# Units, weights and masks at the start of a fused decay-attention and softplus FFN kernel: a new order of loads, a mask on VectorE, a decay table made on the chip

## The chip, the cores and the metric

The kernel runs on one core of a Trainium2 chip. The metric is device time in microseconds (us) of one execution. The engines are TensorE (PE, with its weight loads PEld), VectorE (DVE), ScalarE (ACT), GpSimd (POOL) and SyncE (SP), which here issues nearly all DMAs. Each engine works through its own queue in order, and waits on semaphores where an instruction needs another engine's result or a transfer.

## What is computed

```python
# q, k, v: float32 [4, 8, 768, 64];  w_in: float64 [512, 2048];  w_out: float64 [2048, 512]
gamma = 1.0 - 2.0 ** (-5.0 - np.arange(H))
for t in range(S):
    state = gamma * state + einsum('bhd,bhe->bhde', k[:, :, t], v[:, :, t])
    y[:, :, t] = einsum('bhd,bhde->bhe', q[:, :, t], state) / sqrt(D)
x = y.transpose(0, 2, 1, 3).reshape(3072, 512)
h = x @ w_in
out = (max(h, 0) + log1p(exp(-abs(h)))) @ w_out
```

The attention has a per-head decay and no softmax. The FFN is two matmuls with a softplus between them. The weights come as 64-bit floats and are turned into float32 on the chip.

## The kernel before

**Units.** The attention is done in chunks of 128 tokens, and a unit is one chunk of one batch for four of the eight heads: `units` has 48 of them, unit n being half n % 2 of chunk n // 2. A unit passes through `load_unit` (three loads: q, k, v), `decay` (GpSimd multiplies q and v by decay tables), `operands` (transposes on TensorE, copies to `kz` and `qs`), `scores_whole` or `scores_first`/`scores_second`, the causal `mask`, `new_state` and `stack_and_outputs`, which writes the unit's part of x as a high and a low half (`xh`, `xl`) for the FFN. Units under `WHOLE` = 12 use plain float32 operands and load q and k by tokens; the later units load q and k in 32-token blocks and split them in high and low halves. For a unit under 12 the mask is a copy of the scores from PSUM to `a` on ScalarE (line 268), and then an `affine_select` on GpSimd (line 260).

**Ticks.** `PARTS` says at which tick of a unit each part is traced; unit n is shifted by 16 n. `tick(n)` traces all parts that are due. So unit n is loaded at tick 16 n - 24, its scores are traced at 16 n + 8 (later units at 16 n + 14 and 16 n + 17), and its outputs at 16 n + 20 (26).

**FFN.** A pair is 256 tokens (four units). `turns` and `steps` say which pairs meet which of the 16 blocks of 128 hidden columns: pair 0 with blocks 0 to 7, two blocks a step (steps 0 to 3), pair 1 with all 16 (steps 4 to 11), then pairs 0 and 2 together, and so on. A step is `hidden` (three matmuls for each of the four input tiles: lines 436 to 438), a softplus (lines 444 to 453, over VectorE, ScalarE, VectorE, ScalarE and GpSimd), and two steps later (`LAG`) `second` (lines 471 to 473). Steps 0 to 11 (`ordered`) are ordered by the planner, which works with a cost model of its own; from step 12 on the order on TensorE is the program's.

**Weights.** `load_weights(f)` loads block f of w_in and of w_out, 512 KB each, from SyncE. `convert_weights(f)` turns both into float32 and splits that in two: line 85 on ScalarE, 93 on VectorE or 91 on ScalarE, 94 and 95 on VectorE, the cast of line 97 on ScalarE, the low half of line 98 on GpSimd. The middle result `wp` has one PSUM buffer (tag `acc2`). From block `FETCH` = 3 on, a load is paced: it waits for the cast of the block three before, w_in's for w_in's and w_out's for w_out's. Before the ticks of pair 0 begin, units 0 and 1 are loaded; then the initial loop traces ticks -24 to 79, with block 0's loads in it at the start, block 1's after tick 12, block 2's after 28, and from tick 44 on a conversion and a load every 16 ticks. After that `convert_to` is called around each step.

**Buffers.** The tokens of v have a ring of three buffers, `vns` (unit n takes n % 3). q and k of units 2 and 3 use slots that the softplus takes over later (tags `gh`, `gl`). `attention_bank` gives the transposes, scores and outputs of units under 12 in turn one of two PSUM banks, `acc3` and `a`; later units have only `a`, and the FFN takes `acc3` from pair 2 on.

**Decay tables.** `qtabs` and `vtabs` hold token decays for each chunk and head, the first chunk's loaded and the others made from it (`token_decays`). `qblocks` is the same as `qtabs` in the layout of the later units. Its first chunk is loaded by 16 small DMAs of 0.5 KB (line 538, `block_decays`, called at step `TURN` = 4), and the other chunks are made by ten GpSimd multiplies (line 544).

## Time and profile before

| | us |
|---|---|
| median of three timed runs | 660.43 (659.85 to 660.67) |
| the profiled execution | 661.7 |
| its span, first to last instruction | 660.0 |
| TensorE busy | 648.3 |
| VectorE busy | 411.9 |
| ScalarE busy | 366.7 |
| GpSimd busy | 319.3 |

A timeline row reads: start in us, duration in us, engine, line, operation, what it writes and reads, shape, count; in brackets the idle time of the engine before it and what ended that. A row of the windows view gives a stretch, its length, the busy time of each engine in it, the granted share of TensorE's clock (PEclk), and what the DMA engines did. SPq and ACTq are the engines' sequencers, which issue DMAs. The ends of matmuls are modelled, so a busy TensorE need not be one at its peak.

### The profile page before, as it was taken

The page shows a single profiled execution, that of the slowest core. Times are in us where ns is not written, and L with a number is a line of the kernel's source. Part 1 is how long each engine was busy: PE and PEld are TensorE (multiplying, and loading weights), DVE is VectorE, ACT ScalarE, POOL GpSimd, SP SyncE. Part 2 cuts the span into 40 slices and gives each one's busy share as a digit, 9 for nine tenths or more (in the row PEclk, how much of TensorE's full clock was granted, in tenths as well). Part 3 has the DMA queues.
Part 4 walks back from the last instruction along what each step waited for, and adds up shares of the span by engine and source line. Part 5 has one row for each costly group of instructions (what it writes and reads, how often), then busy time and mean ns, then how long its engine had stood idle before and what let it go on. Part 6 is the DMA issues. An engine that isn't in the chain of part 4 may idle for free.

```text
span 660.0 us, 11777 instructions
## 1 busy us (share of the span) xinstructions
PE 648.3 (98%) x3762; PEld 555.2 (84%) x3762; DVE 411.9 (62%) x756; ACT 366.7 (56%) x799; POOL 319.3 (48%) x330
## 2 busy tenths in 40 slices
PE   7999999999999999999999999999999999999997
PEld 6898899888888888888888888888888888888896
DVE  5777888875685576576566665676677567522221
ACT  5867876656564555556565655565565555422221
POOL 5777758564445445444543464355345543332221
PEclk9999999999999999999999999999999999999999
DMA  9898573132223241131232132131222200000000
GB/s 241 227 260 239 161 195 86 37 76 41 42 62 62 39 96 21 26 84 35 40 84 37 35 92 35 17 82 29 46 61 48 41 19 33 0 1 33 0 33 32
DMA packets 153822, 46.69 MB, mean 71 GB/s; under 512 B 140448, under 2 KB 148640, under 8 KB 153760
## 3 DMA queue, kind: packets, MB, share of 16 engines
q1 hardware_dynamic: 153312, 45.93, 29.3%
q8 instruction: 29, 0.48, 0.3%
q14 instruction: 33, 0.27, 0.1%
q10 hardware_dynamic: 448, 0.01, 0.0%
HBM read 39.60 MB, written 6.29 MB: 70 GB/s over the span
## 4 chain that ended last, share of the span: by engine, by line
PE 92%; DMA 2%; ACT 2%; POOL 1%; issue 0%; DVE 0%; SPq 0%; POOLq 0%; ACTq 0%
PE hp L436 13%; PE hp L438 13%; PE acc L471 13%; PE acc L472 13%; PE hp L437 13%; PE acc L473 13%; PE yp L355 6%; PE sc L280 3%; PE stp L307 2%; DMA win<-in_moe_w_in_dram 2%; PE yp L345 1%; PE sc L267 1%; DMA vn<-in_v_dram 1%; PE yp L342 1%; PE tp L232 0%
## 5 line engine op out<-in xcount | busy, mean ns | idle before, releaser
L453 POOL TENSOR_TENSOR gl<-sp,gh 128x512 fp32r<-128x512 f32 x96 | 129.4, 1349 | 122.5 <-ACT gh L451 118.2
L436 PE MATMUL hp<-xh,winhl 128*128 128x512 f32 (+1 forms) x448 | 166.1, 371 | 1.0 <-DVE sp L449 0.5
L438 PE MATMUL hp<-xh,winhl 128*128 128x512 f32 (+1 forms) x448 | 162.0, 362 | 0.5 <-POOL winhl L98 0.5
L437 PE MATMUL hp<-xl,winhl 128*128 128x512 f32 (+1 forms) x448 | 161.7, 361 | 0.0
L445 ACT ACTIVATE sp<-sp 128x512 f32<-128x512 f32 x96 | 60.7, 632 | 167.7 <-DVE sp L444 167.6
L471 PE MATMUL acc<-wouthl,gh 128*128 128x512 f32 x384 | 151.0, 393 | 0.0
L472 PE MATMUL acc<-wouthl,gh 128*128 128x512 f32 x384 | 150.3, 391 | 0.0
L473 PE MATMUL acc<-wouthl,gl 128*128 128x512 f32 x384 | 149.0, 390 | 0.0
L444 DVE TENSOR_SCALAR sp<-hp 128x512 uint32<-128x512 uint32 x96 | 66.3, 690 | 84.8 <-PE hp L438 62.4
L438 PEld LDWEIGHTS hp<-xh,winhl 128*128 128x128 f32 x448 | 84.5, 189 | 14.3 <-POOL winhl L98 0.9
L436 PEld LDWEIGHTS hp<-xh,winhl 128*128 128x128 f32 x448 | 84.6, 189 | 12.3 <-PE yp L345 0.7
L437 PEld LDWEIGHTS hp<-xl,winhl 128*128 128x128 f32 x448 | 84.8, 189 | 11.2
L451 ACT CAST gh<-sp 128x512 fp32r<-128x512 f32 x96 | 59.7, 621 | 52.1 <-PE acc L472 40.0
L449 DVE SCALAR_TENSOR_TENSOR sp<-hp,sp 128x512 f32<-128x512 f32 x96 | 65.2, 680 | 33.7 <-ACT sp L445 33.2
L260 POOL TENSOR_SCALAR_AFFINE_SELECT a<-a 128x512 f32<-128x512 f32 x48 | 36.6, 762 | 101.6 <-DVE a L281 97.1
L473 PEld LDWEIGHTS acc<-wouthl,gl 128*128 128x128 f32 x384 | 71.8, 188 | 15.1
L471 PEld LDWEIGHTS acc<-wouthl,gh 128*128 128x128 f32 x384 | 72.1, 188 | 12.4
L472 PEld LDWEIGHTS acc<-wouthl,gh 128*128 128x128 f32 x384 | 72.4, 189 | 12.0
L213 POOL TENSOR_TENSOR vn<-vn,vtabs 128x256 f32<-128x256 f32 x48 | 29.8, 621 | 83.6 <-DMA vn<-in_v_dram 71.8
L281 DVE TENSOR_REDUCE a<-sc 128x256 f32<-128x512 f32 x72 | 49.3, 685 | 4.3 <-PE sc L280 3.5
L292 POOL TENSOR_TENSOR al<-a,ah 128x512 fp32r<-128x512 f32 x36 | 47.9, 1331 | 3.1 <-ACT ah L291 3.1
L329 DVE TENSOR_TENSOR st<-stp,st 64x128 fp32r<-64x128 f32 x60 | 17.3, 289 | 44.8 <-ACT st L327 44.2
(94 smaller groups left out, 919.3 us busy)
## 6 DMA issues: line engine op xcount, KB each, us to landing
win<-in_moe_w_in_dram SPq DMA_DIRECT2D x16, 512.0 KB, 4.9
wout<-in_moe_w_out_dram SPq DMA_DIRECT2D x16, 512.0 KB, 4.4
vn<-in_v_dram SPq DMA_DIRECT2D x48, 128.0 KB, 2.8
out_dram<-o SPq DMA_DIRECT2D x24, 256.0 KB, 2.1
vn<-in_k_dram SPq DMA_DIRECT2D x30, 128.0 KB, 2.4
kb<-in_k_dram SPq DMA_DIRECT2D x208, 16.0 KB, 1.7
qb<-in_q_dram SPq DMA_DIRECT2D x208, 16.0 KB, 1.7
qn<-in_q_dram SPq DMA_DIRECT2D x12, 128.0 KB, 4.9
```

The source lines that it names most:

```text
L281: summed[n] = nc.vector.tensor_reduce(sums[n][:, 2 * j:2 * j + 2, :], sc.rearrange("p h t c -> p h c t"), axis=mybir.AxisListType.X, op=AL ...
L436: nc.tensor.matmul(to, lhsT=wt[:, 0, d, :], rhs=xh[:, d], start=d == 0, stop=False)
L437: nc.tensor.matmul(to, lhsT=wt[:, 0, d, :], rhs=xl[:, d], start=False, stop=False)
L438: nc.tensor.matmul(to, lhsT=wt[:, 1, d, :], rhs=xh[:, d], start=False, stop=d == ND - 1)
L444: nc.vector.tensor_scalar(sp.bitcast(U32), hps[s].bitcast(U32), 0x80000000, None, op0=ALU.bitwise_or)
L445: nc.scalar.activation(sp, sp, AF.Softplus)
L449: nc.vector.scalar_tensor_tensor(g, hps.pop(s), 0.0, g, op0=ALU.max, op1=ALU.add)
L451: nc.scalar.copy(gh, g)
L453: nc.gpsimd.tensor_tensor(gl, sps.pop(s), gh.bitcast(F32), op=ALU.subtract)
L471: nc.tensor.matmul(to, lhsT=gh[:, k, ts], rhs=wt[:, 0], start=first, stop=False)
L472: nc.tensor.matmul(to, lhsT=gh[:, k, ts], rhs=wt[:, 1], start=False, stop=False)
L473: nc.tensor.matmul(to, lhsT=gl[:, k, ts], rhs=wt[:, 0], start=False, stop=last)
```

## The change

Seven edits:

1. Units 0 to 2 are loaded first, then the first block of w_in, unit 3, and the second block of w_in. `vns` gets a fourth buffer for unit 3, in a softplus slot (tag `sp`).
2. Weights are loaded and converted as single items in the order of `items`: w_in 0, w_in 1, w_out 0, w_out 1, and from then on w_in and w_out of each block in turn. `FETCH` = 6 items paces each load by the cast six items before. `INITIAL` says how many items are loaded and converted after which tick of the initial loop.
3. A table `causal` (all bits set where the query is not before the key, else zero) is made once, and the mask of units 0 to 3 is one bitwise AND of the scores in PSUM with it on VectorE.
4. `attention_bank` takes the two banks in the other order.
5. The scores of unit 12, the first later unit, are traced at ticks 9 and 13 of the unit, not 14 and 17.
6. The first chunk of `qblocks` is made by ten VectorE copies from `qtabs`; the 16 DMAs are gone.
7. The GpSimd multiplies of `block_decays` are kept in program order.

```diff
@@ -21,12 +22,11 @@
 PLACES = 3
 WIDE = 512
 AHEAD = 9
-EARLY = 2
 WHOLE = 12
 THIRD = 19
 TURN = 4
 LAG = 2
-FETCH = 3
+FETCH = 6
 SLACK = 2.0**-17
 
 
@@ -58,45 +58,48 @@
     vtabs = const.tile([P, NC, H], F32, name="vtabs")
     qblocks = const.tile([P, NC, 2, NJ, C // 32], F32, name="qblocks")
     ident = const.tile([P, P], F32, name="ident")
+    causal = const.tile([P, C], I32, name="causal")
 
 
     raw, win, wout, converts = {}, {}, {}, {}
 
-    def load_weights(f):
+    items = [("win", 0), ("win", 1), ("wout", 0), ("wout", 1)] + [(nm, f) for f in range(2, NF) for nm in ("win", "wout")]
+
+    def load_item(i):
+        nm, f = items[i]
         fs = slice(f * P, (f + 1) * P)
-        raw[f] = [const.tile([P, ND * P], I64, name=nm, tag=f"{nm}{f}") for nm in ("win", "wout")]
-        loads_of_f = (
-            nc.sync.dma_start(raw[f][0].rearrange("p (c w) -> p c w", c=ND), w_in[:, fs].rearrange("(c p) w -> p c w", p=P)),
-            nc.sync.dma_start(raw[f][1], w_out[fs, :]),
-        )
-
-        if f >= FETCH:
-            for load, after in zip(loads_of_f, converts[f - FETCH]):
-                tc.add_manual_dep(load.ins, after.name, mybir.DependencyInfo(mybir.DependencyClass.Sync, mybir.DependencyReason.SCHED_ONLY), reason="pace")
-
-    def convert_weights(f):
-
+        raw[i] = const.tile([P, ND * P], I64, name=nm, tag=f"{nm}{f}")
+        if nm == "win":
+            load = nc.sync.dma_start(raw[i].rearrange("p (c w) -> p c w", c=ND), w_in[:, fs].rearrange("(c p) w -> p c w", p=P))
+        else:
+            load = nc.sync.dma_start(raw[i], w_out[fs, :])
+        if i >= FETCH:
+            paced_by(load, i - FETCH)
+
+    def paced_by(load, i):
+        tc.add_manual_dep(load.ins, converts[i].name, mybir.DependencyInfo(mybir.DependencyClass.Sync, mybir.DependencyReason.SCHED_ONLY), reason="pace")
+
+    def convert_item(i):
         n = ND * P
-        converts[f] = []
-        for nm, bits, to in zip(("win", "wout"), raw.pop(f), (win, wout)):
-            words = bits.bitcast(U32).rearrange("p (n t) -> p n t", t=2)
-            low, high = words[:, :, 0], words[:, :, 1]
-
-            nc.scalar.activation(high.bitcast(F32), high.bitcast(F32), AF.Copy, scale=2.0**-112)
-
-            wp = ps_o.tile([P, n], U32, name="wp", tag="acc2")
-            w = ffn.tile([P, n], U32, name="w", tag="o")
-
-            if nm == "wout":
-                nc.scalar.activation(wp, low, AF.Copy, scale=(1 - SLACK) * 2.0**-29, bias=7.5 * SLACK - 0.5)
-            else:
-                nc.vector.tensor_scalar(wp, low, 29, None, op0=ALU.logical_shift_right)
-            nc.vector.scalar_tensor_tensor(wp, high, 0x80000000, wp, op0=ALU.bitwise_and, op1=ALU.bitwise_or)
-            nc.vector.scalar_tensor_tensor(w, high, 3, wp, op0=ALU.logical_shift_left, op1=ALU.bitwise_or)
-            to[f] = const.tile([P, 2, n], F32R, name=f"{nm}hl", tag=f"{nm}{f}")
-            converts[f].append(nc.scalar.copy(to[f][:, 0], w.bitcast(F32)).ins)
-            nc.gpsimd.tensor_tensor(to[f][:, 1], w.bitcast(F32), to[f][:, 0].bitcast(F32), op=ALU.subtract)
-
+        nm, f = items[i]
+        to = {"win": win, "wout": wout}[nm]
+        words = raw.pop(i).bitcast(U32).rearrange("p (n t) -> p n t", t=2)
+        low, high = words[:, :, 0], words[:, :, 1]
+
+        nc.scalar.activation(high.bitcast(F32), high.bitcast(F32), AF.Copy, scale=2.0**-112)
+
+        wp = ps_o.tile([P, n], U32, name="wp", tag="acc2")
+        w = ffn.tile([P, n], U32, name="w", tag="o")
+
+        if nm == "wout":
+            nc.scalar.activation(wp, low, AF.Copy, scale=(1 - SLACK) * 2.0**-29, bias=7.5 * SLACK - 0.5)
+        else:
+            nc.vector.tensor_scalar(wp, low, 29, None, op0=ALU.logical_shift_right)
+        nc.vector.scalar_tensor_tensor(wp, high, 0x80000000, wp, op0=ALU.bitwise_and, op1=ALU.bitwise_or)
+        nc.vector.scalar_tensor_tensor(w, high, 3, wp, op0=ALU.logical_shift_left, op1=ALU.bitwise_or)
+        to[f] = const.tile([P, 2, n], F32R, name=f"{nm}hl", tag=f"{nm}{f}")
+        converts[i] = nc.scalar.copy(to[f][:, 0], w.bitcast(F32)).ins
+        nc.gpsimd.tensor_tensor(to[f][:, 1], w.bitcast(F32), to[f][:, 0].bitcast(F32), op=ALU.subtract)
 
     units = [(c // NC, c % NC, hf) for c in range(B * NC) for hf in range(2)]
     loads, live, state = {}, {}, {}
...
+
+    vns.append(ffn.tile([P, HH, 2, D], F32, name="vn3", tag="sp"))
+
+    def v_tile(n):
+        return vns[3 if n == 3 else n % 3]
 
 
...
@@ -217,7 +225,7 @@
 
     def attention_bank(n, shape, name):
         taken.append(n)
-        if n < WHOLE and len(taken) % 2:
+        if n < WHOLE and len(taken) % 2 == 0:
             return ps_o.tile(shape, F32, name=name, tag="acc3")
         return ps_a.tile(shape, F32, name=name, tag="a")
 
@@ -265,8 +273,13 @@
         sc = attention_bank(n, [P, HH, C], "sc")
         for h in range(HH):
             nc.tensor.matmul(sc[:, h, :], lhsT=kz[:, h % 2, h // 2, :], rhs=kq[:, h // 2, :], start=True, stop=True)
-        nc.scalar.copy(a, sc)
-        mask(a)
+        if n < 4:
+
+            keep = causal.bitcast(U32).unsqueeze(1).broadcast_to([P, HH, C])
+            nc.vector.tensor_tensor(a.bitcast(U32), sc.bitcast(U32), keep, op=ALU.bitwise_and)
+        else:
+            nc.scalar.copy(a, sc)
+            mask(a)
         live[n].append(a)
 
     sums = {}
@@ -336,7 +349,7 @@
         if n < WHOLE:
             kn, vn, a = rest
             yp = attention_bank(n, [P, NJ, C], "yp")
-            v0 = vns[n % 3].rearrange("p h t d -> p (h t) d")
+            v0 = v_tile(n).rearrange("p h t d -> p (h t) d")
             for j in range(NJ):
                 if c:
                     nc.tensor.matmul(yp[:, j], lhsT=st[:, j, :], rhs=kq[:, j, :], start=True, stop=False)
@@ -388,13 +401,22 @@
     def of_whole(part):
         return lambda n: part(n) if n < WHOLE else None
 
+    def of_rest(part):
+        return lambda n: part(n) if n > WHOLE else None
+
     def of_others(part):
         return lambda n: part(n) if n >= WHOLE else None
 
     PARTS = {-24: of_whole(load_unit), -20: of_others(load_unit), -40: load_ahead, -8: decay, 0: operands}
     PARTS.update({8: of_whole(scores_whole), 12: of_whole(new_state), 20: of_whole(stack_and_outputs)})
-    PARTS.update({14: of_others(scores_first), 17: of_others(scores_second), 18: of_others(new_state), 26: of_others(stack_and_outputs)})
+
+    def of_first(part):
+        return lambda n: part(n) if n == WHOLE else None
+
+    PARTS.update({9: of_first(scores_first), 13: of_first(scores_second), 14: of_rest(scores_first), 17: of_rest(scores_second), 18: of_others(new_state), 26: of_others(stack_and_outputs)})
     FIRST_TICK = -24
+
+    INITIAL = {12: (4, 0), 28: (6, 1), 44: (6, 3), 60: (6, 4), 76: (6, 6)}
     PERIOD = 16
     TICK = 4
     last_tick = PERIOD * (len(units) - 1) + max(PARTS)
@@ -494,18 +516,26 @@
 
     done, loaded, converted = FIRST_TICK, 0, 0
 
+    def load_to(n):
+        nonlocal loaded
+        while loaded < min(len(items), n):
+            load_item(loaded)
+            loaded += 1
+
     def convert_to(n):
-        nonlocal loaded, converted
-        while converted < min(NF, n):
-            convert_weights(converted)
+        nonlocal converted
+        while converted < min(len(items), n):
+            convert_item(converted)
             converted += 1
-            if loaded < NF:
-                load_weights(loaded)
-                loaded += 1
-
-
-    for n in range(2):
+            load_to(converted + FETCH)
+
+
+
+    for n in range(3):
         load_unit(n)
+    load_to(1)
+    load_unit(3)
+    load_to(2)
 
     nc.scalar.dma_start(qtabs[:, 0], qtab)
     nc.scalar.dma_start(vtabs[:, 0], vtab)
@@ -514,6 +544,11 @@
     make_identity(nc, ident)
     for par, own, oth in sides:
         nc.gpsimd.memset(kz[oth, par], 0.0)
+
+    keep = causal.bitcast(F32)
+    nc.gpsimd.memset(keep, -1.0)
+    nc.gpsimd.affine_select(keep, keep, pattern=[[1, C]], compare_op=ALU.is_ge, fill=0.0, base=0, channel_multiplier=-1)
+    nc.vector.tensor_copy(causal, keep)
     for st in stw:
         nc.vector.memset(st, 0.0)
 
@@ -525,6 +560,15 @@
     for kq in kqs:
         for par, own, oth in sides:
             nc.gpsimd.memset(kq[oth, 2, par].bitcast(F32), 0.0)
+
+    for par, half, _ in sides:
+        at = half.start
+        for i in range(C // 32):
+            nc.vector.tensor_copy(
+                qblocks[at:at + 32, 0, :, :, i].rearrange("p f m -> p (f m)"), qtabs[i * 32:(i + 1) * 32, 0, par:H:2]
+            )
+        nc.vector.tensor_copy(qblocks[at + 32:at + 64, 0], qblocks[at:at + 32, 0])
+
     def token_decays():
         nc.vector.reciprocal(gtab_sb[:, 1], gtab_sb[:, 0])
         for c in range(1, NC):
@@ -533,15 +577,11 @@
 
     def block_decays():
         own = (lo, slice(0, H, 2)), (up, slice(1, H, 2))
-        for at in range(0, P, 32):
-            for i in range(C // 32):
-                nc.sync.dma_start(
-                    qblocks[at:at + 32, 0, :, :, i].rearrange("p f m -> p (f m)"), qtab[i * 32:(i + 1) * 32, at // D:H:2]
-                )
         for c in range(1, NC):
             for half, heads in own:
                 old, new = (qblocks[half, t].rearrange("p f m i -> p (f m) i") for t in (c - 1, c))
-                nc.gpsimd.tensor_tensor(new, old, gtab_sb[half, 0, heads].unsqueeze(2).broadcast_to(list(new.shape)), op=ALU.mult)
+                made = nc.gpsimd.tensor_tensor(new, old, gtab_sb[half, 0, heads].unsqueeze(2).broadcast_to(list(new.shape)), op=ALU.mult)
+                tc.keep_in_program_order(made)
 
     while done < ticks_for(0):
         for _ in range(TICK):
@@ -549,12 +589,9 @@
             done += 1
         if done == 3 * TICK:
             token_decays()
-        if done % (4 * TICK) == 3 * TICK and done > 0 or done < 0 and loaded == 0:
-            if loaded >= FETCH:
-                convert_weights(converted)
-                converted += 1
-            load_weights(loaded)
-            loaded += 1
+        if done in INITIAL:
+            load_to(INITIAL[done][0])
+            convert_to(INITIAL[done][1])
 
     ordered = starts[2]
     plan = [0] * ordered
@@ -610,9 +647,10 @@
     for s, (pairs, fs) in enumerate(steps[:ordered]):
         if s == TURN:
             block_decays()
-        convert_to(fs[-1] + 1)
+        assert {("win", f) for f in fs} <= set(items[:converted])
+        assert s < LAG or {("wout", f) for f in steps[s - LAG][1]} <= set(items[:converted])
         stages(s)
-        convert_to((2 * (s + 1) if s < TURN else TURN + s + 2) + EARLY)
+        convert_to(4 * (s + 2) if s < TURN else 4 * (TURN + 1) + 2 * (s + 2 - TURN))
 
     with tc.manual_schedule(engines={mybir.EngineType.PE}):
         for s in range(ordered, len(steps) + LAG):
```

More of the change, by code (lines that the diff above doesn't have):

```diff
@@ L12 @@
 F32R = mybir.dt.float32r
+I32 = mybir.dt.int32
 I64 = mybir.dt.int64
@@ L156, in tokens_of @@
     def tokens_of(n):
-        t = vns[n % 3]
+        t = v_tile(n)
         if n < WHOLE:
```

## The prediction, made before the result was known

> **What bounds the kernel now.** I read the page's totals first, then the windows view (busy time of each engine by stretch), then the chain of waits, and last the timelines of SyncE, ScalarE and GpSimd up to 120 us.
>
> ```profile
> PE 648.3 (98%) x3762; PEld 555.2 (84%) x3762; DVE 411.9 (62%) x756; ACT 366.7 (56%) x799; POOL 319.3 (48%) x330
> ```
> ```profile
> core 0: us, PE busy (x) PEld busy (x) DVE busy (x) ACT busy (x) POOL busy (x), PEclk, DMA share, GB/s
> 0.00:10.00 10.00, 7.88 (x34) 7.04 (x34) 3.52 (x18) 3.15 (x6) 5.44 (x17) 1.00 0.78 200
> 10.00:20.00 10.00, 7.87 (x48) 6.61 (x47) 7.15 (x13) 7.93 (x18) 5.74 (x9) 0.83 1.13 309
> 20.00:30.00 10.00, 9.02 (x67) 7.98 (x68) 7.97 (x16) 8.31 (x19) 7.72 (x9) 1.00 0.81 205
> 30.00:40.00 10.00, 10.00 (x76) 9.42 (x75) 7.80 (x14) 8.81 (x19) 8.56 (x15) 1.00 0.80 207
> 40.00:70.00 30.00, 27.57 (x207) 25.52 (x206) 21.25 (x39) 21.37 (x45) 21.56 (x28) 1.00 0.87 248
> 70.00:110.00 40.00, 40.00 (x275) 36.96 (x274) 33.46 (x56) 31.00 (x61) 29.30 (x28) 1.00 0.59 157
> 110.00:130.00 20.00, 19.79 (x117) 17.03 (x117) 16.52 (x30) 12.47 (x29) 11.34 (x10) 1.00 0.22 42
> 130.00:540.00 410.00, 410.00 (x2332) 346.12 (x2331) 270.64 (x504) 235.23 (x534) 196.85 (x193) 1.00 0.25 51
> ```
>
> TensorE is the bound. From 130 to 540 us it has no idle time at all, and the change touches nothing there. So whatever is won or lost is won or lost before 130 us, and reaches the end one to one. The idle time of TensorE there is 2.12 us in 0:10, 2.13 in 10:20, 0.98 in 20:30, 2.43 in 40:70 and 0.21 in 110:130. A second loss does not show as idle time: part of the start runs at a lower clock.
>
> ```profile
> 15.00:20.00 5.00, 4.10 (x21) 3.36 (x19) 3.67 (x7) 3.77 (x8) 3.46 (x6) 0.66 1.11 307
> 16.62 1.92 PE L267 MATMUL sc<-qs,kz 128*128 128x128 f32 x8
> 35.57 1.06 PE L267 MATMUL sc<-qs,kz 128*128 128x128 f32 x8
> ```
>
> The first row is a window, the others are timeline rows: the same eight score matmuls took 1.92 us where the granted clock was 0.66, and 1.06 us later, so 0.11 us more for each. About 18 matmuls of units 2 and 3 stand in that stretch (4 state, 8 scores, 4 transposes, 2 outputs): 1.9 us, an estimate.
>
> **The change part by part.**
>
> *Term a: units 2 and 3 ahead of the weights, and the shorter mask.*
>
> ```profile
> 8.60 2.44 SPq L70 DMA_DIRECT2D wout<-in_moe_w_out_dram  x1
> 11.08 0.43 SPq L178 DMA_DIRECT2D qn<-in_q_dram  x1
> 12.00 0.61 POOL L206 TENSOR_TENSOR qn<-qn,qtabs 128x256 f32<-128x256 f32 x1 [1.91 <-DMA qn<-in_q_dram]
> 15.94 0.89 PE L307 MATMUL stp<-vn,kn 128*128 128x128 f32 x4 [0.77 <-POOL vn L213]
> 27.64 0.38 ACT L346 CAST xh<-yp 128x256 fp32r<-128x256 f32 x1
> 18.63 0.59 ACT L268 COPY a<-sc 128x512 f32<-128x512 f32 x1 [0.88 <-PE sc L267]
> 19.29 0.64 POOL L260 TENSOR_SCALAR_AFFINE_SELECT a<-a 128x512 f32<-128x512 f32 x1 [0.18 <-ACT a L268]
> ```
> ```profile
> L449 DVE SCALAR_TENSOR_TENSOR sp<-hp,sp 128x512 f32<-128x512 f32 x11 | 7.5, 684 | 0.5 <-ACT sp L445 0.3
> ```
>
> GpSimd waits until 12.00 for the q of unit 2, which stands behind 1.0 MB of weights; unit 3 is issued at 11.08, behind a w_out issue that the full queue held for 2.44 us; its xh is written at 27.64, and only then can the first hidden step finish. Now nine unit DMAs go first. The 1.0 MB ahead of unit 2 cost some 4 us at the 240 to 310 GB/s of these windows, so unit 2 is there by about 8.6 us, and unit 3 (behind 0.5 MB of w_in) by about 12.5. The fourth vn buffer is what lets unit 3 go before unit 0 is done; it borrows a softplus slot, which is first written after unit 3's output anyway, so it costs nothing.
>
> The mask now costs one VectorE pass over PSUM and SBUF. L449 is the same shape of operand: 0.68 us. It replaces 0.59 on ScalarE, 0.64 on GpSimd and the handover: about 0.6 us less on the path of each of units 0 to 3.
>
> Of the 3.1 us idle in 10:30 I take 1.9 as gone, and of the 1.9 us of low clock 1.1. What stays: each unit still goes transposes, kz (one buffer), scores, mask, outputs in turn. So term a is -3.0. Its ends are -5.0 (all of it) and +1.9 (a second stretch at low clock as long as the first).
>
> [...]
>
> *Term b: the decay table on the chip.*
>
> ```profile
> L538 SPq DMA_DIRECT2D qblocks<-in_qtab_dram x16: 565/594/1262, 20.8 to 37.0; - x16
> ```
> ```profile
> 30.66 0.62 ACT L97 CAST winhl<-w 128x512 fp32r<-128x512 f32 x1 [0.42 <-DVE w L95]
> 37.69 0.54 SPq L69 DMA_DIRECT2D win<-in_moe_w_in_dram  x1
> 43.17 0.67 ACT L85 ACTIVATE win<-win 128x512 f32<-128x512 f32 x1 [1.76 <-DMA win<-in_moe_w_in_dram]
> 48.90 0.66 ACT L85 ACTIVATE win<-win 128x512 f32<-128x512 f32 x1 [1.42 <-DMA win<-in_moe_w_in_dram]
> 62.18 0.70 ACT L85 ACTIVATE wout<-wout 128x512 f32<-128x512 f32 x1 [1.85 <-DMA wout<-in_moe_w_out_dram]
> 64.94 0.68 ACT L85 ACTIVATE win<-win 128x512 f32<-128x512 f32 x1 [1.09 <-DMA win<-in_moe_w_in_dram]
> ```
> ```profile
> PE yp L342 <- ACT a L268: 1.5, 2, 1.0
> PE sc L267 <- ACT qs L236: 0.6, 1, 0.6
> PE hp L438 <- POOL winhl L98: 0.5, 2, 0.3
> ```
>
> The first row is the answer for line 538: sixteen issues of some 0.6 us (least, median, most in ns), 9.5 us of SyncE's time between 20.8 and 37.0. SyncE issues there without a pause, while the DMA engines move only about 205 GB/s against 309 before, so the queue's issuing is the limit in 20:40. The w_in load issued at 37.69 was allowed by pacing from the cast at 30.66 on; it could go some 5 us sooner. ScalarE meets that load at 43.17 and the next at 48.90, sits 1.76 and 1.42 us before line 85, and the attention copies behind it on ScalarE keep TensorE waiting. The last rows are of the waits view to 120 us (sum, times, longest): 1.0 us is the longest L342 wait, which lies in this stretch, 0.6 the scores', and 0.3 one of the two waits for a weight's low half (the other is the 0.21 of term c). Of these 1.9 us, within the 2.43 idle in 40:70, I take 1.8 as gone. The waits at 62.18 and 64.94 stay: the loads there are paced by casts six items back, as before. Term b is -1.8, between 0 and -2.43. What is late next is the cast itself.
>
> *Term c: the first later unit and the turned banks.*
>
> ```profile
> 114.98 1.29 POOL L98 TENSOR_TENSOR winhl<-w,winhl 128x512 fp32r<-128x512 f32 x1
> 116.32 0.39 PE L438 MATMUL hp<-xh,winhl 128*128 128x256 f32 x1 [0.21 <-POOL winhl L98]
> ```
>
> The order of unit 12's scores and the bank that unit 11 leaves free can win no more than the 0.21 us that TensorE waits there, and that wait is for a weight's low half. I take -0.2 if the conversions come sooner too, with ends 0 and -0.21. The swap of banks is otherwise symmetric: scores and outputs still alternate.
>
> *Term d: what is added.*
>
> ```profile
> 0.81 0.20 POOL masks.py:197 MEMSET ident<- 128x128 f32 x1 [0.29 <-POOLq L637]
> 2.15 0.29 POOL masks.py:199 TENSOR_SCALAR_AFFINE_SELECT ident<-ident 128x128 f32<-128x128 f32 x1
> 3.56 0.61 POOL L206 TENSOR_TENSOR qn<-qn,qtabs 128x256 f32<-128x256 f32 x1 [0.16 <-DMA qn<-in_q_dram]
> 10.84 0.69 ACT L85 ACTIVATE win<-win 128x512 f32<-128x512 f32 x1
> ```
> ```profile
> L531 DVE TENSOR_TENSOR qtabs<-qtabs,gtab_sb 128x8 f32<-128x8 f32 x5 | 0.8, 151 | 0.0
> ```
>
> The causal table is one more fill and one more select on GpSimd, 0.49 us by the identity's rows, ahead of a multiply that had only 0.16 us of slack: 0.33 us on unit 0's path. Ten small VectorE copies, each nearest to L531 at 0.15 us, are 1.5 us in 3 to 6 us, where VectorE waits for the first transposes; they cost nothing unless the table lands late. The four masks put 2.7 us on VectorE, and each waits for scores, with the next unit's kz half and the weight conversions queued behind it; I charge 0.2. Term d is +0.5; its far end is all 4.2 us of VectorE plus 0.33.
>
> [...]
>
> Sum: -3.0 - 1.8 - 0.2 + 0.5 = -4.5 us. The profiled execution has a span of 660.0 and a time of 661.7 us; its span would become 655.5. The median of the three timed runs, 660.43, becomes 655.9.
>
> **The rivals.**
>
> *Everything goes.* All 5.0 of a, 2.4 of b and 0.2 of c, with 0.2 of cost: 660.4 - 7.4 = 653.0. [...] Against: the units are still chains.
>
> *The transfers stay where they are.* The DMA share in 40:70 is already 0.87, so loads issued sooner may land no sooner. Term b is nothing: 660.4 - 2.7 = 657.7.
>
> *The weight conversions are the pace* (the change does not do what it says). They run from 10.84 to 116.27 as one chain of 32 items, 3.3 us each, and the last but one releases TensorE at 116.32. If that chain does not shorten, TensorE comes earlier and waits there: 660.4.
>
> *The conversions slip,* the slower case. Unit 2's 0.39 MB now stands ahead of the first w_in: 1.4 us at 280 GB/s, and the masks sit among the conversions on VectorE, 2.7 us more. If half of these 4.1 us stays in the chain, its end passes 116.3 by 2 us, and from that point each microsecond is TensorE's: 662.4. Against it: ScalarE and GpSimd lose 4.9 us of mask work, and the 9.5 us of SyncE come back before 40 us.
>
> **How the numbers follow.** A repeated measurement of this kernel can tell about 0.2% (1.3 us) from no change, so faster means below 659.1 and slower above 661.8. Forecast (654.0 to 657.5): 0.50. Everything goes: 0.14. Transfers stay: 0.09. Conversions the pace: 0.12. Conversions slip: 0.15. Faster is 0.50 + 0.14 + 0.09 = 0.73, same 0.12, slower 0.15. The range runs from 651.0, which leaves out the far end of term a, to 661.0, which leaves out the slip: some 0.18 outside.
>
> **What would show it.** Term a: the multiply of unit 2's q starts near 8 us, unit 3's xh before 21 us, TensorE's idle time in 10:30 near 1.2 us. Term b: no qblocks issue, ScalarE's waits at line 85 before 50 us under 1 us in sum. Term c: no idle time near 110 to 116 us. The forecast is wrong if the low half of the last w_in still ends near 116 us with TensorE waiting for it, or if new idle time opens before 70 us where VectorE has a mask ahead of a conversion.

## The result, and the profile after

The changed kernel takes 668.91 us (667.16 to 669.23, four runs) against 660.55 us (659.85 to 661.70, four runs) for the kernel before in the same comparison: a ratio of 1.0121, 95% interval 1.0105 to 1.0136. It is slower, where faster was forecast. Its profiled execution has a span of 665.4 us and a time of 667.16 (before: 660.0 and 661.7); it is the shortest of its four runs, and that of before the longest of its four, so the spans differ by less than the medians.

The page's totals of after:

```profile
PE 648.5 (97%) x3762; PEld 554.9 (83%) x3762; DVE 419.7 (63%) x772; ACT 364.2 (55%) x795; POOL 317.6 (48%) x328
```

TensorE's busy time is that of before but for 0.2 us (648.3), so nearly all of the 5.4 us of span are idle time. The windows view of after, columns as in the prediction, says where:

```profile
0.00:10.00 10.00, 7.15 (x29) 6.19 (x30) 7.84 (x31) 2.28 (x4) 6.57 (x20) 1.00 0.78 182
10.00:20.00 10.00, 9.33 (x69) 8.65 (x68) 7.43 (x15) 5.66 (x15) 2.51 (x3) 1.00 1.12 335
20.00:30.00 10.00, 8.43 (x64) 7.29 (x63) 7.82 (x15) 7.46 (x15) 6.46 (x8) 1.00 0.93 235
30.00:40.00 10.00, 9.41 (x70) 8.66 (x69) 6.39 (x13) 8.50 (x18) 7.72 (x9) 1.00 0.65 192
40.00:70.00 30.00, 28.67 (x213) 26.45 (x212) 22.46 (x41) 22.52 (x48) 21.05 (x23) 1.00 0.77 226
70.00:110.00 40.00, 36.48 (x243) 33.12 (x243) 32.95 (x52) 28.98 (x58) 27.81 (x34) 1.00 0.64 168
110.00:130.00 20.00, 17.47 (x111) 15.35 (x110) 17.75 (x32) 12.84 (x29) 13.03 (x12) 1.00 0.15 30
130.00:540.00 410.00, 410.00 (x2334) 346.27 (x2333) 270.65 (x507) 235.03 (x535) 195.08 (x190) 1.00 0.25 51
...
15.00:20.00 5.00, 4.67 (x38) 4.18 (x38) 4.84 (x10) 3.35 (x9) 1.28 (x1) 1.00 1.13 330
```

Up to 70 us the change is ahead: TensorE was busy 62.99 us against 62.33 and had 435 matmul records against 425 (each kernel's window from 0 to 70 us), and the low clock in 15:20 is gone (1.00 for 0.66). In 70:110, where before had no idle time, it sits 3.52 us, and in 110:130 it sits 2.53 for 0.21. By 130 us it has 785 records for 812 (window from 0 to 130 us). After that the two run alike. So the start was won, and more than that was lost afterwards. The waits view of after to 130 us names what TensorE and ScalarE then wait for (sum, times, longest):

```profile
ACT win L89 <- DMA win<-in_moe_w_in_dram: 6.5, 6, 2.0
...
PE hp L458 <- DVE sp L471: 3.9, 2, 2.3
PE hp L458 <- ACT winhl L101: 2.1, 2, 1.9
...
PE acc L493 <- ACT gh L473: 1.1, 2, 0.6
```

L458 is the first matmul of a hidden block, L101 the cast of a weight's high half, L471 a VectorE pass of the softplus and the last reader of the PSUM buffer `hp`, of which there are two. So of the 6.05 us that TensorE sits in 70:130, 2.1 are waits for a converted weight itself, and 3.9 are waits for VectorE to free a buffer. Timeline rows of after, SyncE, VectorE, GpSimd and ScalarE at the start, then the stalls:

```profile
6.04 0.51 SPq L73 DMA_DIRECT2D win<-in_moe_w_in_dram  x1
...
6.78 0.43 DVE L243 COPY kz<-tp 64x256 f32<-64x256 f32 x1
...
7.58 0.61 POOL L214 TENSOR_TENSOR qn<-qn,qtabs 128x256 f32<-128x256 f32 x1
...
13.84 0.37 ACT L242 COPY kz<-tp 64x256 f32<-64x256 f32 x1 [0.79 <-PE sc L275]
14.11 0.66 ACT L89 ACTIVATE win<-win 128x512 f32<-128x512 f32 x1
...
23.13 0.37 ACT L359 CAST xh<-yp 128x256 fp32r<-128x256 f32 x1 [0.44 <-PE yp L358]
...
48.99 0.70 ACT L89 ACTIVATE win<-win 128x512 f32<-128x512 f32 x1 [0.99 <-DMA win<-in_moe_w_in_dram]
...
72.58 0.36 PE L458 MATMUL hp<-xh,winhl 128*128 128x256 f32 x1 [1.61 <-DVE sp L471]
...
106.52 0.68 ACT L89 ACTIVATE win<-win 128x512 f32<-128x512 f32 x1 [1.82 <-DMA win<-in_moe_w_in_dram]
108.39 0.62 ACT L101 CAST winhl<-w 128x512 fp32r<-128x512 f32 x1
109.06 0.39 PE L458 MATMUL hp<-xh,winhl 128*128 128x256 f32 x1 [1.91 <-ACT winhl L101]
...
120.31 0.62 ACT L101 CAST winhl<-w 128x512 fp32r<-128x512 f32 x1 [1.10 <-DVE w L99]
121.01 1.31 POOL L102 TENSOR_TENSOR winhl<-w,winhl 128x512 fp32r<-128x512 f32 x1 [0.37 <-ACT winhl L101]
...
123.49 0.28 PE L458 MATMUL hp<-xh,winhl 128*128 128x256 f32 x1
...
126.71 1.29 DVE L466 TENSOR_SCALAR sp<-hp 128x512 uint32<-128x512 uint32 x2
128.42 0.69 DVE L471 SCALAR_TENSOR_TENSOR sp<-hp,sp 128x512 f32<-128x512 f32 x1 [0.42 <-ACT sp L467]
...
129.26 0.47 PE L458 MATMUL hp<-xh,winhl 128*128 128x512 f32 x1 [2.30 <-DVE sp L471]
```

The last stall goes back to the last weight all the same. The block of w_in 15 is multiplied from 123.49 to 126.2, after its cast (120.31) and its low half (to 122.32); the softplus passes on it start at 126.71 and 128.42, and the matmul at 129.26 needs its buffer (the profile doesn't number the buffers; this follows if the two take turns). At 72.58 conversions stand in the way: VectorE's first pass (69.31, two of them in 1.28 us) is done near 70, but ScalarE's next, line 467, starts at 71.08, behind two conversion passes (69.95 and 70.52).

And the time from issue to landing of that first w_in load, from the view of DMA issues, of before and of after:

```profile
DMA to landing us min/median/max: 5.5/5.5/5.5
```
```profile
DMA to landing us min/median/max: 4.5/4.5/4.5
```

The load is issued at 6.04 (4.41 before) and lands at 10.5 (9.9 before), 0.6 us later. Its conversion starts only at 14.11, though, because it stands on ScalarE behind the kz copy of unit 2, which waits until 13.84 for scores. Before, it started at 10.84. The chain ends late too: the rows of all w_in casts (least, median, most in ns; first and last start in us), of before and of after, are

```profile
L97 ACT CAST winhl<-w x16: 609/618/624, 13.3 to 112.7; 128x512 fp32r<-128x512 f32 x16
```
```profile
L101 ACT CAST winhl<-w x16: 606/620/622, 17.5 to 120.3; 128x512 fp32r<-128x512 f32 x16
```

The first cast is 4.2 us later, the last 7.6 us later. In between the delay goes up and down. The casts of w_in 3 and w_in 8 of after, and that of w_in 8 of before (w_in 3's is at 30.66 there):

```profile
37.43 0.62 ACT L101 CAST winhl<-w 128x512 fp32r<-128x512 f32 x1
...
69.43 0.62 ACT L101 CAST winhl<-w 128x512 fp32r<-128x512 f32 x1 [0.59 <-DVE w L99]
```
```profile
65.51 0.61 ACT L97 CAST winhl<-w 128x512 fp32r<-128x512 f32 x1
```

It is 6.8 us at w_in 3 and 3.9 at w_in 8: part of what the start loses is made up by 69 us, and lost again where TensorE's stalls lie. At 106.52 ScalarE waits for a load, at 108.39 it casts, and at 109.06 TensorE has waited 1.91 us for that cast.

### The profile page after: what moved, and what is told of

Same layout as the page of the kernel before. It is cut to its first block, busy times and chain, and to the rows that moved or that the text cites. A ratio compares the mean times of both kernels' runs of the same rounds, so it can differ in the third digit from the quotient of the medians.

```text
span 665.4 us, 11755 instructions
## 1 busy us (share of the span) xinstructions
PE 648.5 (97%) x3762; PEld 554.9 (83%) x3762; DVE 419.7 (63%) x772; ACT 364.2 (55%) x795; POOL 317.6 (48%) x328
## 4 chain that ended last, share of the span: by engine, by line
PE 84%; DMA 5%; ACT 4%; issue 3%; DVE 2%; POOL 1%; SPq 0%; POOLq 0%; DVEq 0%; ACTq 0%
PE acc L493 12%; PE acc L494 12%; PE hp L458 12%; PE acc L495 12%; PE hp L460 12%; PE hp L459 12%; PE yp L368 6%; DMA win<-in_moe_w_in_dram 3%; PE sc L293 3%; PE stp L320 2%; DMA kn<-in_k_dram 1%; DMA kb<-in_k_dram 1%; ACT winhl L101 1%; DMA qn<-in_q_dram 1%; DVE w L99 1%
## 5 line engine op out<-in xcount | busy, mean ns | idle before, releaser
L475 POOL TENSOR_TENSOR gl<-sp,gh 128x512 fp32r<-128x512 f32 x96 | 129.7, 1351 | 124.2 <-ACT gh L473 121.1
L458 PE MATMUL hp<-xh,winhl 128*128 128x512 f32 (+1 forms) x448 | 166.4, 372 | 6.0 <-DVE sp L471 3.9
L458 PEld LDWEIGHTS hp<-xh,winhl 128*128 128x128 f32 x448 | 84.6, 189 | 18.1 <-issue 4.2
L471 DVE SCALAR_TENSOR_TENSOR sp<-hp,sp 128x512 f32<-128x512 f32 x96 | 65.3, 680 | 35.8 <-ACT sp L467 35.4
L268 POOL TENSOR_SCALAR_AFFINE_SELECT a<-a 128x512 f32<-128x512 f32 x44 | 34.4, 782 | 104.0 <-DVE a L294 98.0
```

Source lines behind the costliest of these rows:

```text
L458: nc.tensor.matmul(to, lhsT=wt[:, 0, d, :], rhs=xh[:, d], start=d == 0, stop=False)
L471: nc.vector.scalar_tensor_tensor(g, hps.pop(s), 0.0, g, op0=ALU.max, op1=ALU.add)
L475: nc.gpsimd.tensor_tensor(gl, sps.pop(s), gh.bitcast(F32), op=ALU.subtract)
```

## The experiments

Theory 1, formed after the result: loading units 2 and 3 ahead delays the chain of conversions, and its end is TensorE's. Its two forms: 1a, the first weight loads stand too late; 1b, the units' early loads and work take the chain's place. The rivals: the masks on VectorE push the conversions back; the new order of the items does (Theory 3); the later edits around unit 12 cost the stalls near 110 and 130 us (Theory 2). If the conversions aren't the cause at all, making them cheaper changes nothing.

| kernel | median, us | ratio to before [95%] | last w_in cast, us | span, us |
|---|---|---|---|---|
| changed kernel | 668.91 | 1.0121 [1.0105, 1.0136] | 120.3 | 665.4 |
| u6_two_ahead | 662.03 | 1.0008 [0.9992, 1.0023] | 113.2 | 660.2 |
| u1_mask_old | 662.42 | 1.0021 [1.0007, 1.0034] | 114.3 | 660.7 |
| u4_items_old | 664.94 | 1.0051 [1.0031, 1.0071] | 116.5 | 662.9 |
| u2_table_old | 669.26 | 1.0125 [1.0098, 1.0153] | 121.8 | 666.4 |
| u3_first_old | 669.19 | 1.0119 [1.0098, 1.0140] | 121.1 | 668.3 |
| b4_ahead_alone | 669.46 | 1.0135 [1.0107, 1.0164] | 121.5 | 668.6 |
| b6_weights_before_unit2 | 663.87 | 1.0045 [1.0030, 1.0061] | 117.1 | 663.5 |
| b1_mask_alone | 660.90 | 1.0007 [0.9993, 1.0021] | 112.7 | 659.7 |
| b2_table_alone | 658.21 | 0.9968 [0.9948, 0.9988] | 110.1 | 656.5 |
| v1_fetch8 | 664.72 | 1.0054 [1.0037, 1.0072] | 115.5 | 662.6 |
| v2_after_light | 662.02 | 1.0013 [1.0001, 1.0025] | 92.0 | 660.2 |
| v3_before_light | 662.64 | 1.0031 [1.0017, 1.0046] | 85.7 | 660.5 |
| b5_before_fetch4 | 662.29 | 1.0031 [1.0016, 1.0046] | 113.5 | 659.5 |
| c2_mask_old_fetch8 | 660.61 | 1.0006 [0.9995, 1.0016] | 113.5 | 660.6 |
| c3_two_fetch8 | 662.79 | 1.0039 [1.0025, 1.0053] | 108.6 | 661.1 |
| b7_table_fetch4 | 658.76 | 0.9964 [0.9949, 0.9978] | 108.6 | 656.4 |

The kernels whose name begins with b, and v3, are edits of the kernel before; the others are edits of the changed kernel. The casts are the last start in the row of each kernel's w_in casts; casts and spans are of the profiled executions. The comparisons' medians of the kernel before run from 660.35 to 661.23, so differences under 1 us between rows say nothing.

### One edit undone

**u6_two_ahead: only units 0 and 1 before the weights**

```diff
-    for n in range(3):
+    for n in range(2):
         load_unit(n)
-    load_to(1)
-    load_unit(3)
     load_to(2)
```

> The changed kernel with units 0 and 1 alone ahead of the weights; units 2 and 3 are loaded at their own ticks again, the rest of the change stays. Theory 1 (the chain of weight conversions is the pace, and it slips at the start because four units' loads, copies and masks stand before the first conversion): the first w_in cast, at 17.5 us in the changed kernel and 13.4 before, comes back to 13 to 15 us, the last w_in cast (120.3 against 112.7) to 116 or less, and the time falls from 668.9 to 662 to 665. Theory 2 (the loss is made late, by the order around unit 12 and the turned banks, where TensorE stands still at 106.8 and 126.7 us): 667 to 670, with the waits at 106.8 and 126.7 still there. Theory 3 (the new order of w_in and w_out): 667 to 670.

The time is that of before again, and so is the chain, from its first cast on:

```profile
L101 ACT CAST winhl<-w x16: 606/620/623, 14.3 to 113.2; 128x512 fp32r<-128x512 f32 x16
```

Theory 1 holds here. The fourth buffer for v is still in this kernel, so it isn't what costs. All the other edits together, with this one undone, gain nothing either.

**u1_mask_old: the copy and select for units 0 to 3, no table of bits**

```diff
-        if n < 4:
...
-        else:
-            nc.scalar.copy(a, sc)
-            mask(a)
+        nc.scalar.copy(a, sc)
+        mask(a)
```

> The changed kernel with the old mask for units 0 to 3 (a copy on ScalarE, a select on GpSimd) and no causal table. Theory 1, if the four masks on VectorE (0.69 us each) are a good part of the slip: the first w_in cast comes from 17.5 to about 16 us, the last from 120.3 to about 118, the time to 665 to 667. If the loads alone are the cause: no sooner first cast, 668 to 670, since the units' own path is 0.6 us longer each. Theory 2: 667 to 670.

6.5 us better than the changed kernel, more than any theory gave it; the first cast is at 15.9 for 17.5, the last at 114.3. Units 2 and 3 are still ahead, so Theory 1 in its plain form doesn't say why.

**u4_items_old: w_in and w_out of each block in turn from the first on**

```diff
-    items = [("win", 0), ("win", 1), ("wout", 0), ("wout", 1)] + [...]
+    items = [(nm, f) for f in range(NF) for nm in ("win", "wout")]
...
-    INITIAL = {12: (4, 0), 28: (6, 1), 44: (6, 3), 60: (6, 4), 76: (6, 6)}
+    INITIAL = {12: (4, 0), 28: (6, 0), 44: (6, 2), 60: (6, 4), 76: (6, 6)}
```

> The changed kernel with w_in and w_out of blocks 0 and 1 in the old order (w_in 0, w_out 0, w_in 1, w_out 1). Theory 1: the first cast stays at about 17.5 us and the time at 667 to 669. Theory 3 (w_in 1 ahead of w_out 0 holds up the chain: the cast of w_in 2 is at 31.5 us against 25.0 before): the cast of w_in 2 comes to 28 us or less and the time falls to 662 to 665. Theory 2: 667 to 670.

4.0 us better, in the range of Theory 3 and below that of Theory 1 (667 to 669). But the early part that Theory 3 looks at hardly moved (the third w_in cast, w_in 2's, starts at 31.0 for 31.5 us, not by 28); the last cast is 3.8 us sooner. So neither theory is borne out.

**u2_table_old: the sixteen DMAs again, no copies**

```diff
-    for par, half, _ in sides:
-        at = half.start
...
+        for at in range(0, P, 32):
+            for i in range(C // 32):
+                nc.sync.dma_start(
...
```

> The changed kernel with the first chunk of the decay table by 16 small DMAs again. The prediction's term b (they cost 1.8 us by holding up SyncE's queue): 670 to 671. If the ten VectorE copies, which put unit 0's kz copy at 6.8 us against 5.8 before, cost more than the DMAs: 666 to 668. Theory 1 alone: the first cast at 16.5 to 17.5 us, 667 to 670.

No difference. On top of four units ahead the table's gain is hidden. The first cast starts at 15.6, 1.9 us sooner than in the changed kernel, and the last at 121.8, 1.5 later: an earlier first cast alone buys nothing.

**u3_first_old: unit 12 at its old ticks, the old parity of the banks**

```diff
-        if n < WHOLE and len(taken) % 2 == 0:
+        if n < WHOLE and len(taken) % 2:
...
-    PARTS.update({9: of_first(scores_first), 13: of_first(scores_second), ...})
+    PARTS.update({14: of_others(scores_first), 17: of_others(scores_second), ...})
```

> The changed kernel with unit 12's scores at their old ticks and the two banks in the old order. Theory 1: w_in 3's cast stays at 36 to 38 us and the time at 667 to 670. Theory 2 (the wait of 2.4 us at 126.7 comes from unit 12's scores standing sooner): the wait at 126.7 us goes, and the time falls to 665 to 667.

No difference, and the waits remain: to 140 us TensorE waits 3.3 us for the softplus, 1.74 of them up to 132.02, and 2.2 for a w_in cast. These edits are neither gain nor cause.

### One edit alone, on the kernel before

**b4_ahead_alone: units 0 to 3 loaded first, with the fourth buffer**

```diff
+    vns.append(ffn.tile([P, HH, 2, D], F32, name="vn3", tag="sp"))
...
-    for n in range(2):
+    for n in range(4):
         load_unit(n)
```

> The kernel before with one part of the change alone: units 0 to 3 all loaded first, with the fourth vn buffer; masks, table, order of weights and pacing as before. Theory 1 (data of units ahead of the weights makes the conversion chain slip): the first w_in cast comes after 16 us (13.3 before), w_in 3's cast after 34 us (30.7), and the time is 662 to 666. If the order alone is harmless and the slip needs the masks on VectorE as well: w_in 3's cast by 32 us, and 659 to 662. The prediction's term a alone would give 657 to 658.

This edit alone makes the whole loss: 669.46 against 660.35 in its comparison, +9.1 us. (It goes a little further than the change, where w_in 0 stands ahead of unit 3.) First the row of its waits view, then of its w_in casts:

```profile
ACT win L85 <- DMA win<-in_moe_w_in_dram: 13.2, 11, 2.4
```
```profile
L97 ACT CAST winhl<-w x16: 604/619/626, 17.7 to 121.5; 128x512 fp32r<-128x512 f32 x16
```

ScalarE waits 13.2 us for w_in loads to 130 us, 8.7 before, and the chain has the changed kernel's delay at both ends, with the old mask and the old order. It is more than any of the theories gave. TensorE's waits, from the same view, and three timeline rows:

```profile
PE yp L346 <- ACT a L272: 3.1, 3, 1.8
PE yp L349 <- POOL a L264: 2.1, 5, 0.9
...
PE hp L442 <- POOL winhl L98: 1.4, 2, 0.8
...
PE hp L440 <- ACT winhl L97: 1.1, 1, 1.1
```
```profile
71.62 0.67 ACT L85 ACTIVATE wout<-wout 128x512 f32<-128x512 f32 x1 [0.57 <-DMA wout<-in_moe_w_out_dram]
...
73.11 0.58 ACT L272 COPY a<-sc 128x512 f32<-128x512 f32 x1
...
73.75 0.49 PE L346 MATMUL yp<-qs,stw 128*128 128x128 f32 x2 [1.76 <-ACT a L272]
```

Of 14.4 us idle before 130 us, 2.5 are waits for halves of w_in, and 5.2 for the mask's copy on ScalarE and its select on GpSimd. The longest of these shows how the two hang together: the copy of the scores stands on ScalarE behind a conversion that waits for its load, and TensorE waits for the copy.

**b6_weights_before_unit2: as b4, but block 0's weights between units 1 and 2**

```diff
-    for n in range(4):
+    for n in range(2):
+        load_unit(n)
+    load_weights(loaded)
+    loaded += 1
+    for n in 2, 3:
         load_unit(n)
```

> The kernel before with units 0 and 1, then block 0 of w_in and w_out, then units 2 and 3, all at the start; the fourth vn buffer as in the run with four units ahead (669.5). Theory 1a (what costs is that the first weights land behind the data of units 2 and 3, so that the first conversion is queued behind those units' copies): the first w_in cast is at 13 to 14.5 us, w_in 3's by 33 us, the time 659 to 663. Theory 1b (the early work of units 2 and 3 itself crowds the conversions out, wherever the weights stand): w_in 3's cast after 35 us and 664 to 670.

663.87: some 5.6 us of b4's 9 are back, 3.4 remain. The first cast starts at 13.2, as before, w_in 3's at 33.7, which like the time lies between what 1a and 1b said, and the last at 117.1. So both forms have a share: the place of the first loads (1a) the larger, what units 2 and 3 take afterwards (1b) the rest.

**b1_mask_alone: the AND mask**

```diff
+        if n < 4:
+            keep = causal.bitcast(U32).unsqueeze(1).broadcast_to([P, HH, C])
+            nc.vector.tensor_tensor(a.bitcast(U32), sc.bitcast(U32), keep, op=ALU.bitwise_and)
...
```

> The kernel before with the mask on VectorE for units 0 to 3 alone. The prediction had 0.6 us less on each unit's path and 0.2 us of cost: 658.5 to 660.5. Theory 1 (VectorE work among the first conversions makes the chain slip): w_in 3's cast 1 to 3 us later than 30.7, and 661 to 664.

The time is that of before (the interval holds 1). The early chain does slip as Theory 1 said, w_in 3's cast is at 32.6 for 30.7, but that is made up: w_in 8's is at 63.3 for 65.5, and the last at 112.7 as before.

**b2_table_alone: the decay table on the chip**

```diff
+            nc.vector.tensor_copy(
+                qblocks[at:at + 32, 0, :, :, i].rearrange("p f m -> p (f m)"), qtabs[i * 32:(i + 1) * 32, 0, par:H:2]
+            )
...
-                nc.sync.dma_start(
...
```

> The kernel before with the decay table made on the chip alone: no small DMAs in SyncE's queue. The prediction's term b: 1.8 us less, 658 to 659.5, with ScalarE's waits for w_in near 43 and 49 us gone. If the limit is elsewhere, as undoing it in the changed kernel says (669.3 against 668.9): 660 to 661.5, even with those waits gone.

658.21 against 660.49, -2.3 us, with the interval clear of 1: faster than both kernels. Its windows view has 0.14 us of idle time in 40:70 (2.43 before), and on ScalarE the two w_in items that waited 1.76 and 1.42 us start without a wait:

```profile
40.00:70.00 30.00, 29.86 (x228) 28.32 (x227) 24.26 (x44) 24.52 (x52) 23.94 (x27) 1.00 0.77 224
...
40.34 0.69 ACT L85 ACTIVATE win<-win 128x512 f32<-128x512 f32 x1
...
45.31 0.67 ACT L85 ACTIVATE win<-win 128x512 f32<-128x512 f32 x1
```

### The conversions' pace

**v1_fetch8: loads paced by the cast eight items back**

```diff
-FETCH = 6
+FETCH = 8
```

> The changed kernel with each weight load paced by the cast eight items before, not six. If the chain is slow because each load waits for a cast and lands 4 to 5 us later (ScalarE waits 8.8 us in all for weights at line 89): the twelve blocks from w_in 3's cast to w_in 15's take 78 us or less (82.9 in the changed kernel), and the time is 663 to 666. If the chain is held by the engines' own queues: 81 to 84 us, and 667 to 670. The slip up to w_in 3's cast (37.4 us against 30.7 before) should stay either way.

4.2 us better. The first cast is at 18.4, later than in the changed kernel, the last at 115.5, 4.8 us sooner, and TensorE's idle time in 70:110 is gone. Only the pacing of the weight loads was touched, and the end follows it. By w_in 8 the delay against before is 1.8 us here, 3.9 in the changed kernel.

**v2_after_light and v3_before_light: a shorter conversion, in both kernels**

```diff
-            nc.scalar.activation(wp, low, AF.Copy, scale=(1 - SLACK) * 2.0**-29, bias=7.5 * SLACK - 0.5)
...
-        nc.vector.scalar_tensor_tensor(wp, high, 0x80000000, wp, op0=ALU.bitwise_and, op1=ALU.bitwise_or)
-        nc.vector.scalar_tensor_tensor(w, high, 3, wp, op0=ALU.logical_shift_left, op1=ALU.bitwise_or)
+        nc.vector.tensor_scalar(w, high, 3, None, op0=ALU.logical_shift_left)
```

> The changed kernel with a lighter weight conversion: the sign and the lowest three bits of each weight are left out, so that one VectorE pass per item stands where three (w_in) or two and a ScalarE pass (w_out) stood. Its partner is the kernel before with the same cut. Theory 1 (the conversion chain is the pace: in the runs so far the span follows the last w_in cast, span minus cast 544.6 to 547.3 us): with the chain lightened the changed kernel loses its waits at 106.8 and 126.7 us and falls from 668.9 to 655 or less, and what the prediction's term a won at the start shows again: it is level with its partner or up to 4 us faster. Theory 2 (the loss is made by the order of the units and softplus passes late in the start): it stays 5 us or more slower than its partner.

> The kernel before with the same cut of the conversion (sign and lowest three bits of each weight left out). Theory 1: it falls little, 655 to 659, since the kernel before hardly waits for conversions from 70 us on. Theory 2: the same fall, and the changed partner 5 us or more above it.

With the chain over by 92.0 and 85.7 us the two kernels are level, 662.02 and 662.64: the change's loss is gone with the conversions as pace. The times that Theory 1 gave (655 or less, and 655 to 659) are missed: neither gets below the kernel before, which the lighter conversion makes slower by 1.4 us (ratio 1.0031). And the cut takes passes from the queues of VectorE and ScalarE too, so the pair can't tell waits for weights from waits behind conversions. The 40:70 windows, of v2 and of v3, show what is left:

```profile
40.00:70.00 30.00, 28.35 (x203) 26.04 (x203) 21.05 (x31) 24.46 (x51) 27.59 (x30) 1.00 0.88 258
```
```profile
40.00:70.00 30.00, 27.18 (x185) 24.47 (x185) 19.00 (x28) 22.33 (x47) 27.47 (x32) 1.00 0.98 291
```

1.65 and 2.82 us idle there, with the DMA share at 0.88 and 0.98, and 8.1 and 9.3 us in all before 130 us. So there is a second limit close behind the first.

**b5_before_fetch4: the kernel before with loads paced four blocks back**

```diff
-FETCH = 3
+FETCH = 4
...
-            if loaded >= FETCH:
+            if done > 10 * TICK:
```

> The kernel before with each weight load paced by the cast four blocks before, not three. If pacing is a part of the conversion chain's length whatever the start: the twelve blocks from w_in 3's cast to w_in 15's, 82.0 us before, take 77 to 79 us, as with the deeper pacing in the changed kernel (77.9). TensorE is idle for no more than 2.6 us from 40 us on in the kernel before, so the time gains 0 to 2.5 us at most: 658 to 661. If deeper pacing only robs the units' loads: slower than 661.

The last cast moved from 112.7 to 113.5, not forward, and the kernel is 1.9 us slower (ratio 1.0031). The gain of v1 doesn't carry over to a chain that starts on time.

### Together

**c2_mask_old_fetch8, c3_two_fetch8, b7_table_fetch4: two of these edits at once**

```diff
-FETCH = 6
+FETCH = 8
```

with the old mask (c2) or with two units ahead (c3); b7 is b2 with b5's edit.

> The changed kernel with the old mask and with loads paced eight items back. If the two repairs act on different parts of the chain (the mask on its start, 37.4 to 34.0 us at w_in 3's cast; pacing on its rate, 82.9 to 77.9 us for the last twelve blocks) they add up: last w_in cast near 112 us, and with the start that the units have won (first hidden step done at 27.5 against 30.9 us before) 655 to 659. If TensorE is bound elsewhere by then (the units' own chain): 660 to 663, with its idle time before 130 us still 7 to 9 us.

> The changed kernel with two units ahead of the weights, not four, and loads paced eight items back. The two repairs adding up: last w_in cast near 109 us, 656 to 660. If the units' own chain bounds TensorE by then: 660 to 663.

> The kernel before with the table made on the chip and loads paced four blocks back. If the two add: the last w_in cast by 110 us (112.7 before) and 657 to 659. If TensorE's idle time in the first 30 us and the units' chain are a floor: 660 to 662.

c2 comes level with before at 660.61 and not below. c3 has its last cast at 108.6, 4.1 us sooner than before, and still takes 662.79: its end is not the conversions'. b7 ends the chain 1.5 us sooner than b2 and is no faster (658.76 against 658.21). Below the kernel before are b2 and b7 alone, which are that kernel without its small DMAs. u6 and c3 have no small DMAs and no units ahead either, but also the mask, the order and pace of single items and the edits around unit 12, and stay 0.4 and 0.7% above b2 (2.6 and 4.7 us by the table's ratios); which of these takes it wasn't separated.

## Why the prediction was wrong

**The step that failed** is term a, -3.0 us: it priced what TensorE wins when units 2 and 3 are loaded first, and put down nothing for what the weight conversions lose by it. Loading the four units first, with all else as before, costs 9.1 us (b4), and with that alone undone the loss of 8.4 is gone (u6). The rival that the conversions slip had the loss, with a chance of 0.15 and 2 us, but from a transfer and the masks. The transfer lands 0.6 us later, not 1.4. The masks cost nothing by themselves (b1), close to the 0.2 that term d charges for work queued behind them, though undoing them in the whole mends 6.5 us (u1). What nothing in the working priced is the first w_in's place in ScalarE's queue: it waits there 3.6 us after landing (0.9 before), 13.84 standing ahead of 14.11. The delay is 6.8 us by w_in 3, and the chain makes up only a part of it for a time.

**How the delay reaches TensorE** is seen in part. The span less the last w_in cast is 544.6 to 547.8 us in 15 of the 16 kernels with the whole conversion, before (660.0 - 112.7 = 547.3) and after (665.4 - 120.3 = 545.1) among them; c3, at 552.5, is the exception. That is a correlation over runs, and it doesn't say which leads, since casts and the units' copies share queues and a late TensorE holds up both. That units ahead make the loss is shown by b4 and u6; that the chain's pace has a part in it, by v1; the light pair fits. TensorE's waits for weights themselves are the smaller part (2.1 of 6.05 us from 70 us on, 2.5 of 14.4 in b4). Others are for softplus and mask passes behind conversions in the queues of ScalarE and VectorE (the rows at 72.58 here and 73.75 in b4). How much each way takes, no run tells.

**Term a** had its mechanism: q of unit 2 at 7.58 (said: near 8), low clock gone from the profiled execution (mean 0.999; the other three of the changed kernel have 0.994 to 0.997). The size was less: 2.24 us idle in 10:30, not 1.2, xh of unit 3 at 23.13, not before 21, and 0.73 us more idle in 0:10. The 2.44 us of the w_out issue ahead of unit 3 are measured (the one at 4.96 took 0.50); that a full queue held it is the author's reading, which no row shows. What was won is spent after 70 us, where TensorE's waits follow work that comes later. (The prediction's eight score matmuls are four, one for each head, which the profile shows as eight records; its estimate counts records throughout and stands.) The low clock had little to give anyway. In the four comparisons of the experiments, 68 of the 88 executions of the kernel before (one of 1661.8 us left out) have a mean granted clock of 0.999 or 1.000, with a median of 660.5 us. The other 20 are at 0.996 or 0.997 (the profiled one has 0.997), with a median of 660.9 us. That is 0.4 us, where the term took 1.1 of an estimated 1.9 as won, in a stretch that, by their clocks, most executions don't have. In the profiled one the windows of 1 us from 16 to 20 have 0.67, 0.50, 0.50 and 0.62, and 15:16 and 20:21 have 1.00; the profiled execution of after has 1.00 in all of 15:20. What lowers the clock in some executions and not in others, no run shows.

**Term b** was right by itself: -2.3 against -1.8 (b2), with the idle time gone from 40:70 where it was said to go, and in the changed kernel too ScalarE's waits at line 89 before 50 us are one, 0.99 us. There it brings nothing (u2); that later stalls absorb it is likely but not shown. **Term c** is nothing (u3). In **term d** the causal table cost what was said (unit 0's multiply starts at 3.86 for 3.56), and the small copies, priced at nothing, put unit 0's kz copy 0.9 us back.

**The sum** took the terms as additive. They are not: undoing the units ahead, the mask or the order of items recovers 6.9, 6.5 and 4.0 us, some 17 together, of 8.4 lost. Each edit lets the planner order every queue anew. Why the old mask or the old order mends a kernel with four units ahead, while b4 has both and loses all, stays open. What makes the second limit near 660 us is open too. The kernels that stop there (u6, u1, v2, v3) are idle for 8 to 10 us before 130 us, but so is b7 (8.2), which is faster.

## What to carry to other kernels

Before moving loads ahead at a start, find the longest chain that begins there, and follow its first item not only to its landing but through the queue of the engine that takes it; then compare the last item's time, since a gain at the start pays only if that doesn't move. An earlier first item alone decides nothing, as u2 and b6 show. Many tiny DMAs in a busy issuing queue can be worth removing, even where each costs only 0.6 us (2.3 us here). Where a planner reorders everything, a part's worth alone and its worth within the whole are two measurements; make both.

## What the runs showed of the hardware

The small VectorE copies were not free for unit 0: without them (u2) its kz copy on VectorE starts at 5.84, with them at 6.78. The answer of after for line 567 (least, median, most in ns; first and last start), and its timeline on VectorE and GpSimd:

```profile
L567 DVE COPY qblocks<-qtabs x8: 158/164/799, 3.2 to 6.4; 32x4 f32<-32x4 f32 x8
```
```profile
3.69 0.80 DVE L567 COPY qblocks<-qtabs 32x4 f32<-32x4 f32 x1
...
3.86 0.61 POOL L214 TENSOR_TENSOR qn<-qn,qtabs 128x256 f32<-128x256 f32 x1
```

The copy that started at 3.69 lasted 0.80 us where the median is 0.164, and it ends at 4.49, just after GpSimd's multiply (3.86 + 0.61 = 4.47), which kept its usual length (median of its line 0.613). Two later passes of VectorE do the same beside GpSimd multiplies of after:

```profile
7.58 0.61 POOL L214 TENSOR_TENSOR qn<-qn,qtabs 128x256 f32<-128x256 f32 x1
7.75 0.47 DVE L576 TENSOR_TENSOR vtabs<-vtabs,gtab_sb 128x8 f32<-128x8 f32 x1
...
8.46 0.64 POOL L221 TENSOR_TENSOR vn<-vn,vtabs 128x256 f32<-128x256 f32 x1 [0.26 <-DVE vtabs L576]
8.53 0.58 DVE L575 TENSOR_TENSOR qtabs<-qtabs,gtab_sb 128x8 f32<-128x8 f32 x1
```

Others of these two lines last 0.15 to 0.17 us; these end at 8.22 and 9.11, 0.03 and 0.01 us after GpSimd's (8.19 and 9.10). In these two GpSimd's start is ahead of VectorE's, by 0.17 and 0.07 us; the copy starts 0.17 us before the multiply and is still the one that is longer. In all three it is VectorE's pass that is longer, while GpSimd's take 0.61, 0.61 and 0.64 us (medians of their lines 0.613 and 0.615). That the one waited for the other is read from equal ends; no run tried it alone, and none shows why.
